# One more product of the last stage split into seven smaller products, and one more slice in seven of its weight sums added by transfers

## The chip, the cores and the metric

The kernel runs on one core of a Trainium2 chip. The metric is the device time of one execution in microseconds (us). TensorE (PE in the profile) multiplies, VectorE (DVE) adds and subtracts tensors, ScalarE (ACT) copies and applies functions, GpSimd (POOL) and SyncE (SP) here only issue transfers (DMAs).

## What is computed

The reference is a gated mix of two branches over a 2048 x 1024 input. Branch a is the real part of a two-dimensional Fourier transform, written as matrix products. Branch b is a token-mixing MLP: LayerNorm, a product with w1 (2048 x 3584), GELU, a product with w2 (3584 x 2048), with biases. A sigmoid gate of each row mixes them.

```python
g = sigmoid((x * gate_w).sum(-1, keepdims=True))
a = real(dft_seq @ (x @ dft_hid.T))
h = layernorm(x)
u = gelu(einsum("bsd,sf->bdf", h, w1) + b1)
b = transpose(einsum("bdf,fs->bds", u, w2) + b2)
return g * a + (1 - g) * b
```

The change touches the product with w2 alone, the last stage.

## The kernel before, in words

The kernel runs four stages one after the other: two for the Fourier branch (`FastSeq`, `FastHid`), then `Up` (the product with w1 and the GELU) and `Down` (the product with w2, line 1384). It keeps float32 accuracy by splitting each operand into a high part `hi` and a rest `lo`, both of the format fp32r, and by multiplying three times: hi by hi, hi by lo and lo by hi. ACT makes `hi` (line 666), DVE makes `lo` as the difference (line 673, or line 671 where the sign of the operand is turned at the same time). A plain matmul is 128 x 128 weights by 512 columns (lines 1069 to 1071).

`Up` and `Down` are of the class `Bilinear` (line 740). The matrices are cut in blocks: in `Down` the weights w2 (called W) are 4 x 4 blocks of 896 x 512, the stored result u of `Up` (called R) is 4 x 2 blocks of 896 x 512, and the output is 4 x 2 blocks. A fixed table, `SCHEME`, computes the 32 block products as 26 products of signed sums of blocks. `O_ORDER` (line 244) gives the order of the 26 products; product j here is the j-th in that order. `plan` chooses by which additions the sums are made and which sums stay in SBUF for the next products (`O_KEEP`) or go to a buffer in HBM.

One product has seven slices k of 128 rows (`nk` = 7), four groups m of 128 output rows (`nm` = 4) and 512 columns: 7 x 4 x 3 = 84 matmuls. Its result stands in four PSUM banks, which DVE or ACT then read into accumulators (`read`; lines 1114 and 1122). A product can be chained to the one before, and then goes on in the same banks.

Two tuples and a method steer what the change is about:

- `O_NEST` (line 282) lists the products that are made in the nested way (`nested`, line 921): the first six of the seven slices form a 2 x 2 scheme of quarters, which takes seven smaller products in place of eight. Each of the seven has three slices, two groups of output rows, 256 columns and three passes: 18 matmuls of 256 columns. ACT first writes zeros into the halves of the banks that begin an accumulation (`zero`, line 967), copies two halves (line 987), and DVE adds shared halves in PSUM (line 992). The operands of the seven are quarters or sums of quarters: four sums of three quarter-slices for R (names `_s`) and four for W (names `_t`), and each operand is split into hi and lo. The seventh slice is done in the plain way. Before the change, products 3, 15 and 22 are nested.
- `by_dma` (line 1393) says which block sums are made by a transfer that adds, in place of an addition on DVE. It holds for products j above 1 in the slices k with (k + j) mod 7 in `O_DMA` (line 278), and for all slices of the products in `O_MADE` (line 279). `operand` (line 845) uses it where one of the two terms is still in HBM, the other may be overwritten, and the signs agree: the other term stays where it lies, and `add_onto` (line 641) issues on POOL a DMA that adds the first one onto it. Otherwise both terms are loaded by SP (line 639) and DVE adds or subtracts (lines 631 and 634).

The order of all instructions is not written by hand. `Graph.schedule` places each task on its engine by its own cost figures, by due times that it takes from the order of TensorE's work, and by free slots: `SLOTS` gives 39 buffers of 4 KB per partition ("f"), 24 of 2 KB ("h") and 8 PSUM banks. The order found when the kernel is built is fixed; each engine then runs its list in that order and waits on semaphores. So each engine can be ahead of TensorE as far as buffers, loads and its own speed allow.

Of the kernel before, what the change touches and what calls it, by code (L numbers as in the profile page):

```python
# [274 lines left out]


O_KEEP, O_AHEAD = 2, 7
O_DMA = (1, 4, 6)
O_MADE = (3, 6, 9, 21, 22, 23)
U_MADE = (0, 1)  # L280
O_GAP = 99
O_NEST = (3, 15, 22)
O_CLOSE = ((0, 6), (0, 7), (0, 9), (1, 7), (1, 10), (1, 12), (1, 13), (1, 20), (1, 22), (2, 2), (2, 5), (2, 12), (2, 13), (2, 14), (2, 18), (2, 21), (2, 23), (3, 1), (3, 2), (3, 3), (3, 4), (3, 8), (3, 9), (3, 13), (3, 15), (3, 19), (3, 20), (4, 1), (4, 4), (4, 18), (4, 19), (4, 20), (5, 0), (5, 7), (5, 10), (5, 15), (5, 17), (5, 20), (5, 22), (6, 1), (6, 4), (6, 7), (6, 9), (6, 11), (6, 13), (6, 15), (6, 18), (6, 19))
Y_NEST = ()
O_PERM = ((0, 1, 2, 3), (0, 1, 2, 3), (0, 1))
# [277 lines left out]
def arm(  # L563
# [176 lines left out]
    class Bilinear:  # L740
# [90 lines left out]
        def by_dma(self, x, j, k, o):  # L831
            return False
# [551 lines left out]
    class Down(Bilinear):  # L1384
        pairs = True
        nest, close = O_NEST, O_CLOSE
        gap = O_GAP
# [5 lines left out]
        def by_dma(self, x_, j, k, o):  # L1393
            return j > 1 and (k + j) % 7 in O_DMA or j in O_MADE

# [1057 lines left out]
```

## Time and profile before

| what | value |
|---|---|
| time, median of 3 runs | 1230.14 us (1228.32 to 1230.95) |
| the profiled execution's own time | 1229.13 us |
| span in its profile | 1227.3 us (1.8 us lie around it) |
| granted TensorE clock | 0.999 |
| TensorE busy | 1212.1 us, 99% of the span |
| DVE busy | 1150.9 us, 94% |
| ACT busy | 703.7 us, 57% |
| POOL busy | 210.4 us, 17% |
| first and last matmul of `Down` | 725.6 us and about 1219 us |

A row of the profile's groups names the line, the engine, the operation, what is written and read (buffer numbers left out), the shape and the count, then busy time and mean duration. In the timeline a row is a start and a duration in us; in square brackets stands how long the engine was idle before it and what released it. Rows in the timeline that follow each other on one engine can overlap: the spacing of their starts says how fast the engine takes such instructions. Names that begin with `o_` or `ps_o` belong to `Down`, with `u_` or `ps_u` to `Up`.

### The profile page before, as it was taken

The page shows a single profiled execution, that of the slowest core. Times are in us where ns is not written, and L with a number is a line of the kernel's source. Part 1 is how long each engine was busy: PE and PEld are TensorE (multiplying, and loading weights), DVE is VectorE, ACT ScalarE, POOL GpSimd, SP SyncE. Part 2 cuts the span into 40 slices and gives each one's busy share as a digit, 9 for nine tenths or more (in the row PEclk, how much of TensorE's full clock was granted, in tenths as well). Part 3 has the DMA queues.
Part 4 walks back from the last instruction along what each step waited for, and adds up shares of the span by engine and source line. Part 5 has one row for each costly group of instructions (what it writes and reads, how often), then busy time and mean ns, then how long its engine had stood idle before and what let it go on. Part 6 is the DMA issues. An engine that isn't in the chain of part 4 may idle for free.

```text
span 1227.3 us, 17616 instructions
## 1 busy us (share of the span) xinstructions
PE 1212.1 (99%) x5640; PEld 979.4 (80%) x5647; DVE 1150.9 (94%) x1989; ACT 703.7 (57%) x1262; POOL 210.4 (17%) x325
## 2 busy tenths in 40 slices
PE   9999999999999999999999999999999999999997
PEld 6578756778888888888887878988888889888986
DVE  8999979999998899979999899899999889999995
ACT  8852699565843434645656556655535546765632
POOL 0000010312130221312312132102110112231302
PEclk9999999999999999999999999999999999999999
DMA  9999882989587799999998999778984678899655
GB/s 374 403 335 408 289 254 92 292 295 380 200 285 267 261 355 394 367 408 409 415 379 312 396 398 275 216 235 223 258 269 143 169 186 230 232 260 282 134 133 106
DMA packets 142281, 347.35 MB, mean 283 GB/s; under 512 B 17377, under 2 KB 20321, under 8 KB 142178
## 3 DMA queue, kind: packets, MB, share of 16 engines
q1 hardware_dynamic: 109762, 256.39, 58.0%
q0 software_dynamic: 32272, 89.67, 26.6%
q8 instruction: 46, 0.75, 0.3%
q14 instruction: 57, 0.47, 0.1%
q10 hardware_dynamic: 144, 0.07, 0.0%
HBM read 264.40 MB, written 81.66 MB: 282 GB/s over the span
## 4 chain that ended last, share of the span: by engine, by line


## 5 line engine op out<-in xcount | busy, mean ns | idle before, releaser
L1071 PE MATMUL ps_u_p<-u_p_r_hi,u_p_w_lo 128*128 128x512 f32 x728 | 283.5, 389 | 1.8 <-DVE u_p_w_lo L671 1.8
L1070 PE MATMUL ps_u_p<-u_p_r_lo,u_p_w_hi 128*128 128x512 f32 x728 | 283.3, 389 | 1.2 <-DVE u_p_r_lo L673 1.2
L1069 PE MATMUL ps_u_p<-u_p_r_hi,u_p_w_hi 128*128 128x512 f32 x728 | 283.7, 390 | 0.3 <-DVE u_c L1122 0.2
L1069 PE MATMUL ps_o_p<-o_p_r,o_p_w 128*128 128x512 f32 x654 | 255.0, 390 | 0.6 <-DVE u_c L1122 0.6
L1070 PE MATMUL ps_o_p<-o_p_r,o_p_w 128*128 128x512 f32 x654 | 254.5, 389 | 0.0
L1071 PE MATMUL ps_o_p<-o_p_r,o_p_w 128*128 128x512 f32 x654 | 254.4, 389 | 0.0
L1071 PEld LDWEIGHTS ps_u_p<-u_p_r_hi,u_p_w_lo 128*128 128x128 f32 x728 | 136.7, 188 | 31.1 <-DVE u_p_w_lo L671 2.7
L1070 PEld LDWEIGHTS ps_u_p<-u_p_r_lo,u_p_w_hi 128*128 128x128 f32 x728 | 136.7, 188 | 29.6 <-DVE u_p_r_lo L673 1.6
L1069 PEld LDWEIGHTS ps_u_p<-u_p_r_hi,u_p_w_hi 128*128 128x128 f32 x728 | 136.7, 188 | 29.4 <-DVE u_c L1122 1.1
L666 ACT ACTIVATE u_p_w_hi<-u_W_p 128x896 fp32r<-128x896 f32 x104 | 97.9, 950 | 105.9 <-DVE u_W_p L631 33.3
L1069 PEld LDWEIGHTS ps_o_p<-o_p_r,o_p_w 128*128 128x128 f32 x654 | 122.8, 188 | 28.2 <-DVE u_c L1122 1.9
L666 ACT ACTIVATE o_p_r<-o_R_p 128x512 fp32r<-128x512 f32 x157 | 96.5, 626 | 84.8 <-DVE o_R_p L634 39.8
L1071 PEld LDWEIGHTS ps_o_p<-o_p_r,o_p_w 128*128 128x128 f32 x654 | 122.8, 188 | 25.4
L1070 PEld LDWEIGHTS ps_o_p<-o_p_r,o_p_w 128*128 128x128 f32 x654 | 122.8, 188 | 25.1
L666 ACT ACTIVATE o_p_w<-o_W_p 128x512 fp32r<-128x512 f32 x164 | 100.6, 625 | 61.1 <-DVE o_W_p L634 28.3
L673 DVE TENSOR_TENSOR o_p_r<-o_R_p,o_p_r 128x512 fp32r<-128x512 f32 x157 | 106.4, 683 | 2.2 <-ACT o_p_r L666 2.2
L1122 DVE SCALAR_TENSOR_TENSOR u_c<-ps_u_p,u_c 128x512 f32<-128x512 f32 x161 | 104.7, 683 | 1.1 <-PE ps_u_p L1071 0.7
L649 POOL DMA_DIRECT2D u<-u_c x126 | 68.7, 545 | 198.7 <-DVE u_c L1122 111.1
L1623 PE MATMUL ps_fq<-fc,fx_f 128*128 128x256 f32 (+1 forms) x368 | 100.3, 417 | 2.2 <-DVE fx_f L631 2.1
L644 POOL DMA_DIRECT2D o_W_p<-in_w_dram x50 | 45.3, 930 | 266.1 <-DVE o_p_w L671 68.0
L1623 PEld LDWEIGHTS ps_fq<-fc,fx_f 128*128 128x128 f32 x368 | 69.4, 190 | 26.4 <-issue 12.4
L631 DVE TENSOR_TENSOR u_W_p<-u_W_p,u_W_p 128x896 f32<-128x896 f32 x72 | 76.7, 1085 | 10.9 <-DMA u_W_p<-in_w_dram 10.8
(291 smaller groups left out, 1982.8 us busy)
## 6 DMA issues: line engine op xcount, KB each, us to landing
u_W_p<-in_w_dram SPq DMA_DIRECT2D x124, 448.0 KB, 7.9
o_W_p<-in_w_dram SPq DMA_DIRECT2D x160, 256.0 KB, 5.8
o_R_p<-u SPq DMA_DIRECT2D x140, 256.0 KB, 5.7
fc<-in_ct_dram SPq DMA_DIRECT2D x64, 512.0 KB, 9.2
u<-u_c POOLq DMA_DIRECT2D x126, 256.0 KB, 6.4
u_c<-u SPq DMA_DIRECT2D x70, 256.0 KB, 8.5
o_W_p<-in_w_dram POOLq DMA_DIRECT2D x50, 256.0 KB, 6.9
out_dram<-o_c POOLq DMA_DIRECT2D x44, 256.0 KB, 7.9
```

The costliest lines, as they stand in the source:

```text
L631: g.add({"DVE": dve(o.n)}, key, lambda e: nc.vector.tensor_add(o.ap, a.ap, b.ap), r=(a.reg, b.reg), w=(o.reg,))
L644: g.add({"POOL": 0.9}, key, lambda e: nc.gpsimd.dma_start(dst(), src, accum_op=ALU.add), r=(v.reg, *r), w=(v.reg,), nbytes=2.2 * P * v.n * 4)
L649: g.add({queue: 0.6 if queue == "POOL" else 0.06}, key, lambda e: q.dma_start(dst, v.ap), r=(v.reg,), w=(reg,) if reg else (), nbytes=P * ...
L666: g.add({"ACT": act(v.n)}, key, lambda e: nc.scalar.activation(hi.ap, v.ap, AF.Copy, scale=-1.0 if negate else 1.0), r=(v.reg,), w=(hi.reg,))
L673: nc.vector.tensor_sub(lo.ap, v.ap, hi.ap.bitcast(F32))
L1069: nc.tensor.matmul(bank.ap, wh.ap[:, c], rh.ap[:, e], start=a, stop=False, skip_group_check=True)
L1070: nc.tensor.matmul(bank.ap, wh.ap[:, c], rl.ap[:, e], start=False, stop=False, skip_group_check=True)
L1071: nc.tensor.matmul(bank.ap, wl.ap[:, c], rh.ap[:, e], start=False, stop=b, skip_group_check=True)
L1122: lambda e: nc.vector.scalar_tensor_tensor(o.ap, ps.ap, scale, o.ap, op0=ALU.mult, op1=ALU.add),
L1623: nc.tensor.matmul(b.ap[:, c0:c0 + r.shape[-1]] if r.shape[-1] < H else b.ap, w, r, start=begin, stop=end, skip_group_check=True)
```

## The change

```diff
-O_DMA = (1, 4, 6)
+O_DMA = (1, 3, 4, 6)
...
-O_NEST = (3, 15, 22)
+O_NEST = (0, 3, 15, 22)
```

Product 0, the first one of `Down`, becomes nested like products 3, 15 and 22. Its operands are single blocks: W block 9 and R block 2, with no block sums. And in the products that `by_dma` covers by slice, four slices of seven are asked to be made by adding transfers, where it was three. No other line differs; the order of all engines' work is found anew from the same rules.

## The prediction

> **What bounds the kernel now.** I read the page first: the span and the busy time of the engines.
>
> ```profile
> span 1227.3 us, 17616 instructions
> ...
> PE 1212.1 (99%) x5640; PEld 979.4 (80%) x5647; DVE 1150.9 (94%) x1989; ACT 703.7 (57%) x1262; POOL 210.4 (17%) x325
> ```
>
> TensorE is busy nearly always, DVE almost as long. The page's chain that ended last is empty here, so I go by stretches of the last stage: the 22.6 us before its first matmul, products 0 to 2, product 3 up to 960 us, then the rest. The columns are the length, then busy time and instructions of PE, weight loads, DVE, ACT and POOL, the clock, the share of the DMA engines and GB/s.
>
> ```profile
> 703.00:725.60 22.60, 22.60 (x102) 18.64 (x101) 20.74 (x35) 7.37 (x13) 4.88 (x10) 1.00 1.04 391
> 725.60:784.40 58.80, 58.17 (x253) 46.98 (x253) 54.95 (x106) 39.58 (x78) 14.30 (x21) 1.00 0.89 277
> 784.40:960.00 175.60, 175.60 (x834) 147.68 (x834) 174.26 (x290) 96.17 (x170) 22.20 (x28) 1.00 0.75 220
> 960.00:1012.00 52.00, 52.00 (x231) 43.05 (x230) 43.79 (x82) 22.26 (x41) 7.79 (x9) 1.00 0.75 193
> 1012.00:1219.00 207.00, 206.98 (x1034) 176.48 (x1033) 197.66 (x348) 120.94 (x220) 48.45 (x55) 1.00 0.79 201
> ```
>
> PE never waits in the last stage except at its start (58.17 of 58.80), so PE's own work sets the end. But DVE has 1.3 us of idle time in the 175.6 us from 784.4 on, and 8.2 us in the 52 us after that. It is a second bound just behind the first. ACT has room everywhere; the DMA engines are full (1.04) until PE begins the stage.
>
> How far DVE is ahead of PE decides what more DVE work costs. Product 3 is nested and its operands have names of their own (`_s`, `_t`, `_hi`, `_lo`), so its rows can be told apart. First the timeline of PE: the first matmul of the stage and the thirteenth, the first of product 3 and the first one behind its nested part, and two matmuls 33 apart in plain products.
>
> ```profile
> 725.59 0.39 PE L1069 MATMUL ps_o_p<-o_p_r,o_p_w 128*128 128x512 f32 x1
> ...
> 729.80 0.39 PE L1069 MATMUL ps_o_p<-o_p_r,o_p_w 128*128 128x512 f32 x1
> ...
> 784.44 0.28 PE L980 MATMUL ps_o_p<-o_p_r_hi,o_p_w_hi 128*128 128x256 f32 x1
> ...
> 799.55 0.40 PE L1069 MATMUL ps_o_p<-o_p_r,o_p_w 128*128 128x512 f32 x1
> ...
> 1187.57 0.39 PE L1069 MATMUL ps_o_p<-o_p_r,o_p_w 128*128 128x512 f32 x1
> ...
> 1195.05 0.39 PE L1069 MATMUL ps_o_p<-o_p_r,o_p_w 128*128 128x512 f32 x1
> ```
>
> Then DVE's timeline: its first work for the stage, its waits, and how fast it takes instructions.
>
> ```profile
> 703.00 2.50 DVE L673 TENSOR_TENSOR o_p_w<-o_W_p,o_p_w 128x512 fp32r<-128x512 f32 x4
> ...
> 712.10 0.69 DVE L631 TENSOR_TENSOR o_W_p<-o_W_p,o_W_p 128x512 f32<-128x512 f32 x1 [0.82 <-DMA o_W_p<-in_w_dram]
> ...
> 719.24 0.69 DVE L634 TENSOR_TENSOR o_R_p<-o_R_p,o_R_p 128x512 f32<-128x512 f32 x1 [0.88 <-DMA o_R_p<-u]
> ...
> 730.06 0.68 DVE L671 SCALAR_TENSOR_TENSOR o_p_w<-o_W_p,o_p_w 128x512 fp32r<-128x512 f32 x1
> ...
> 742.70 0.68 DVE L671 SCALAR_TENSOR_TENSOR o_p_w<-o_W_p,o_p_w 128x512 fp32r<-128x512 f32 x1
> ...
> 753.53 0.68 DVE L673 TENSOR_TENSOR o_p_r<-o_R_p,o_p_r 128x512 fp32r<-128x512 f32 x1
> 754.13 0.68 DVE L673 TENSOR_TENSOR o_p_w<-o_W_p,o_p_w 128x512 fp32r<-128x512 f32 x1
> ...
> 757.75 1.08 DVE L631 TENSOR_TENSOR o_p_r_s<-o_R_p,o_R_p 128x256 f32<-128x256 f32 x3
> 758.75 1.09 DVE L634 TENSOR_TENSOR o_p_w_t<-o_W_p 128x256 f32<-128x256 f32 x3
> ...
> 763.79 0.94 DVE L673 TENSOR_TENSOR o_p_r_lo<-o_p_r_s,o_p_r_hi 128x768 fp32r<-128x768 f32 x1
> 764.66 0.94 DVE L673 TENSOR_TENSOR o_p_w_lo<-o_p_w_t,o_p_w_hi 128x768 fp32r<-128x768 f32 x1
> ...
> 773.95 0.69 DVE L631 TENSOR_TENSOR o_W_p<-o_W_p,o_W_p 128x512 f32<-128x512 f32 x1 [0.78 <-DMA o_W_p<-in_w_dram]
> 775.21 0.69 DVE L631 TENSOR_TENSOR o_W_p<-o_W_p,o_W_p 128x512 f32<-128x512 f32 x1 [0.56 <-DMA o_W_p<-in_w_dram]
> ...
> 784.03 0.96 DVE L673 TENSOR_TENSOR o_p_w_lo<-o_p_w_t,o_p_w_hi 128x768 fp32r<-128x768 f32 x1 [2.50 <-PE ps_o_p L1071]
> 784.90 1.09 DVE L673 TENSOR_TENSOR o_p_r_lo<-o_R_p,o_p_r_hi 128x256 fp32r<-128x256 f32 x3
> ```
>
> DVE begins product 3's operands at 757.75, 26.7 us before PE begins the product. The last one, the quarter for the last of the seven smaller products, is ready at 784.90 + 1.09 = 786.0. PE wants it six smaller products after 784.44: the nested part takes 799.55 - 784.44 = 15.11 us, a seventh is 2.16, so at 784.44 + 12.95 = 797.4. DVE is 11.4 us ahead there. Product 1 turns the sign of its W operands: its seven W splits are the seven L671 rows from 730.06 to 742.70, so its last one is ready at 743.4. PE wants it with the sixth slice of product 1. Product 0 ends at 729.80 + 72 x 0.2267 = 746.1 (the pace is worked out below), five slices of 2.72 go before, so at 759.7: DVE is 16.3 us ahead.
>
> **PE's part.** A plain matmul of 512 columns is taken every (1195.05 - 1187.57) / 33 = 0.2267 us. Six plain slices are 72 matmuls, 16.32 us. Nested they are 7 x 18 = 126 matmuls of 256 columns in 15.11 us, 0.120 each. So product 0's matmuls get shorter by 1.2 us and no more: an eighth of the multiplying is saved, but half the columns cost 53% of the time. The Trainium skill, "TensorE: Matmul & The Clock Gate", section "Back-to-back issue gap", gives an isolated gap of columns / 2.4 + 2.5 ns, so an estimate of 215.8 and 109.2 ns: by it the nested form would save 15.54 - 13.76 = 1.8 us. The trace disagrees on the small matmul (120 ns), and the sum goes by the trace.
>
> At the start of the stage there is a second gain. From 725.59 to 729.80 stand 12 matmuls, which need 2.72 us and took 4.21: 1.5 us are lost while DVE reads the banks of the last product of `Up`. A plain product wants its four banks 0.68 us apart; the nested one works 18 matmuls (2.16 us) on two banks before it needs the third. Against that, ACT must write zeros into each bank once DVE has read it:
>
> ```profile
> L967 ACT ACTIVATE ps_o_p<-const-bfloat16-1.0 x12: 359/372/382, 729.6 to 1070.9; 128x256 f32<-128x256 bf16 x12
> ```
>
> That is 0.37 us and a hand-over more per bank. The three late banks were there 1.0, 2.2 and 3.4 us after the start; with 0.5 us more each they come at 1.5, 2.7 and 3.9, and are wanted at 1.1, 2.2 and 3.2. About 0.7 of the 1.5 us stays. Gain 0.8, bounds 0 and 1.5. PE's own part is -1.2 - 0.8 = -2.0 us.
>
> **DVE's part.** The counts behind the nested operands, over three nested products:
>
> ```profile
> L673 DVE TENSOR_TENSOR o_p_w_lo<-o_p_w_t,o_p_w_hi 128x768 fp32r<-128x768 f32 x12 | 11.4, 946 | 2.5 <-PE ps_o_p L1071 2.5
> ...
> L673 DVE TENSOR_TENSOR o_p_w_lo<-o_W_p,o_p_w_hi 128x256 fp32r<-128x256 f32 x27 | 10.1, 412 | 0.0
> ```
>
> So one nested product has 4 wide and 9 quarter splits for W and as many for R, and by the code 4 x 3 sums for each, and 4 additions in PSUM. By the spacing of starts three 256-wide instructions take 1.00 us (757.75 to 758.75) and a 768-wide one 0.87 (763.79 to 764.66). Sums 24 x 0.335 = 8.0, quarter splits 18 x 0.335 = 6.0, wide splits 8 x 0.87 = 7.0, in PSUM 4 x 0.335 = 1.3: 22.4 us. It takes the place of 12 plain splits at 0.60 (753.53 to 754.13), 7.2 us. DVE gets 15.2 us more, all before or within the first product. ACT gets 18 quarter and 8 wide `hi` splits in place of 12 plain ones:
>
> ```profile
> L666 ACT ACTIVATE o_p_w_hi<-o_p_w_t 128x768 fp32r<-128x768 f32 x12 | 10.1, 840 | 3.3 <-DVE o_R_p L634 2.3 <-DVE o_p_w_t L634 0.5 <-DVE o_p_r_lo L673 0.5
> ...
> L666 ACT ACTIVATE o_p_w_hi<-o_W_p 128x256 fp32r<-128x256 f32 x27 | 9.4, 405 | 0.3 <-PE ps_o_p L1071 0.3
> ```
>
> 18 x 0.405 + 8 x 0.84 = 14.0 us gross, and ACT is idle for 15.2 of the 22.6 us before the stage: no cost, unless ACT's work comes later than that.
>
> **The adding transfers.** I counted by the rule in `operand`, product by product; the same count for the kernel before gives 160 W loads and 50 adding W transfers, as the rows below have them. After, there are 12 more adding transfers (61 for W, one for R), 12 fewer sums on DVE, 11 fewer W loads and one reload less. DVE saves 12 x 0.60 = 7.2 us, spread thin: products 2 and 4 lose one sum each, product 5 two, products 8 and 10 one each, the other six lie from product 15 on.
>
> ```profile
> o_W_p<-in_w_dram SPq DMA_DIRECT2D x160, 256.0 KB, 5.8
> ...
> o_W_p<-in_w_dram POOLq DMA_DIRECT2D x50, 256.0 KB, 6.9
> ```
>
> An adding transfer must follow the load of the other term, so such a sum takes 5.8 + 6.9 us from the first issue, where two loads side by side and an addition took some 7. SP issues less and POOL 12 more; POOL is 17% busy. From product 2 on the DMA share is 0.75 to 0.89. I take no cost, and bound it by one late landing of 6.9 us less the lead of DVE, so again by DVE's lead.
>
> **What the lead pays.** For product 3's last operand: ready at 786.0 + 15.2 - 0.6 (product 2's sum) = 800.6, if DVE waits as before. PE wants it at 797.4 - 2.0 = 795.4. DVE's five waits on the way are 0.82 + 0.88 + 0.78 + 0.56 + 2.50 = 5.5 us. If a later DVE finds all of these loads landed and buffers free, it is ready at 795.1, in time by 0.3; if it keeps all five, PE waits 5.2. The three waits from 773 on I count as gone (DVE comes 10 us later to them), of the two before 720 half: 4.7 us filled, 0.5 us of PE wait. Product 1 is nearer to safe: 16.3 - 15.2 - 2.0 plus the 1.7 us leaves 0.8. After product 3 DVE is nearly level with PE, and a hand-over that the lead used to hide is then seen. The nearest row is nested product 22, where PE lost time in the middle:
>
> ```profile
> 1150.48 0.28 PE L980 MATMUL ps_o_p<-o_p_r_hi,o_p_w_lo 128*128 128x256 f32 x1
> 1150.77 0.39 PE L980 MATMUL ps_o_p<-o_p_r_hi,o_p_w_hi 128*128 128x256 f32 x1
> 1150.99 0.28 PE L980 MATMUL ps_o_p<-o_p_r_lo,o_p_w_hi 128*128 128x256 f32 x1
> ```
>
> 0.29 and 0.22 in place of 0.12 twice, 0.27 us; for two such places, products 0 and 3, I take 0.5. Bounds: 0, and the 5.2 above. From there on six sums fewer and the 8.2 us idle after 960 give DVE its lead back, so nothing is added later.
>
> Sum: -2.0 + 0.5 + 0.5 = -1.0 us. On the profiled execution that is 1229.13 - 1.0 = 1228.1. That execution stands 1.0 below the median of the runs shown, 1230.14, so the forecast for the median is 1229.1. The measurement can tell about 0.2%, 2.5 us, from no change.
>
> **Rivals.** *DVE becomes the bound at the front of the stage.* For it: 15.2 us more work against 11.4 us of lead, and only 1.3 us of slack in the next 175. Against it: the waits that a later DVE can fill. It decides once more than 0.3 us of the five waits stay; with all five, -2.0 + 5.2 = +3.2, 1233.3. Slower. Chance 0.22, of which two thirds beyond 0.2%.
>
> *Buffers run out at the change of stages.* The nested product needs 28 full-size split buffers over its life in place of 12 for six plain slices, while `Up` still holds its own. The 28 loads of product 1 then come later: the DMA share is 1.04 there at 391 GB/s, so 0.67 us per 256 KB load, and 14 loads held back are 9.4 us. Of product 1's remaining 0.8 us nothing stays: +8.6 - 2.0 = +6.6, 1236.7. The trace shows no buffer wait of DVE before 784.03, which speaks against so much. Chance 0.06. The Trainium skill, "Perfetto Trace Analysis", section "Optimization Strategy", says that gaps which repeat on the engine that should be full can mean too little SBUF; no run here shows it yet.
>
> *All of the cover holds.* The 1.5 us at the banks vanish, no new wait comes, and the sums saved late take away the 0.27 us in product 22: -1.2 - 1.5 - 0.3 = -3.0, 1227.1. Chance 0.12, nearly all of it beyond 0.2%.
>
> The forecast case, -2.0 to +2.0, has 0.60. The change does what it says by the count above; I give nothing to the opposite.
>
> **The numbers.** Faster by over 0.2%: 0.10, from the third rival. Slower: two thirds of 0.22 and most of 0.06, some of the forecast's upper edge, 0.24. Within: 0.66. The range reaches from the third rival, 1227.1 less a little for the spread of the runs, 1226.8, to the first rival's 1233.3 and a little more, 1234.5; the second is left out.
>
> **What would show it.** In the changed profile there should be 504 matmuls of 256 columns at line 980, the first of them at the start of the stage, and 15.1 us until line 1069 follows; 61 adding W transfers; 12 fewer DVE sums at lines 631 and 634; a gap at the first banks of 0.7 us. PE's waits between 745 and 800 should be about 1 us in sum. If they are 4 us or more with DVE named, the first rival is right; if DVE itself waits there for loads or for PE, the second. DVE should be idle for less than 3 us in the 52 us before product 15. The forecast is wrong if the stage starts later than 725.6: then `Up` was disturbed, which no term here holds.

## The result, and the profile after

| what | before | after |
|---|---|---|
| time, median | 1229.80 us (4 runs, 1228.32 to 1230.95) | 1241.84 us (4 runs, 1237.77 to 1242.40) |
| ratio | | 1.0094 [1.0074, 1.0115] |
| profiled execution, span | 1229.13, 1227.3 us | 1242.40, 1240.5 us |

The change makes the kernel slower by 0.94%. The forecast was a gain of 1.0 us, 1229.1, with a range from 1226.8 to 1234.5; the sign was wrong, and the time lies above the range. Here is the page of the kernel after, span and engines:

```profile
span 1240.5 us, 17800 instructions
...
PE 1215.7 (98%) x5701; PEld 984.7 (79%) x5701; DVE 1159.1 (93%) x2019; ACT 712.0 (57%) x1284; POOL 220.2 (18%) x337
```

TensorE's busy time grows by 3.6 us and the span by 13.2, so most of the loss is waiting, which the shares of the page do not show. DVE has 8.2 us more work, close to the 15.2 - 7.2 = 8.0 of the prediction, and 30 instructions more: nested operands bring 24 + 18 + 8 + 4 = 54 in place of 12, and 12 sums go. The DMA issues of the same page answer to the two rows of the prediction:

```profile
o_W_p<-in_w_dram SPq DMA_DIRECT2D x149, 256.0 KB, 6.0
...
o_W_p<-in_w_dram POOLq DMA_DIRECT2D x61, 256.0 KB, 7.4
```

The counts are those forecast, 11 loads fewer and 11 adding transfers more, and each lands a little later (6.0 and 7.4 us in place of 5.8 and 6.9).

Next the windows of the kernel after: the 24.9 us ahead of the stage, then nested product 0, the plain ones after it, nested product 3, plain ones, nested 15, and the rest. The columns are as in the prediction.

```profile
703.00:727.90 24.90, 24.90 (x111) 20.62 (x110) 18.67 (x40) 7.98 (x17) 3.24 (x6) 1.00 0.88 328
727.90:749.06 21.16, 17.18 (x128) 16.67 (x126) 19.92 (x40) 15.80 (x34) 4.83 (x9) 0.92 0.81 281
749.06:790.07 41.01, 41.01 (x183) 33.72 (x181) 40.69 (x78) 27.90 (x54) 12.07 (x16) 1.00 0.93 250
790.07:806.37 16.30, 15.37 (x128) 15.17 (x127) 14.31 (x32) 12.48 (x27) 1.73 (x2) 1.00 0.80 224
806.37:1018.59 212.22, 212.22 (x939) 175.63 (x937) 204.01 (x345) 107.29 (x190) 34.30 (x42) 1.00 0.78 220
1018.59:1038.92 20.33, 17.01 (x127) 16.70 (x126) 19.05 (x41) 15.14 (x32) 1.73 (x2) 0.92 0.49 162
1038.92:1231.23 192.31, 192.31 (x914) 161.74 (x912) 181.63 (x316) 107.80 (x193) 49.66 (x57) 1.00 0.82 199
```

All that TensorE loses in the stage lies in three nested products. Product 0 takes 21.16 us, product 3 takes 16.30 and product 15 takes 20.33, where a nested part took 15.11 before. The plain products between them have no wait at all. And in two rows the granted clock is 0.92. TensorE's timeline in the kernel after shows where:

```profile
727.90 0.28 PE L980 MATMUL ps_o_p<-o_p_r_hi,o_p_w_hi 128*128 128x256 f32 x1
...
732.09 0.28 PE L980 MATMUL ps_o_p<-o_p_r_hi,o_p_w_lo 128*128 128x256 f32 x1
733.75 0.39 PE L980 MATMUL ps_o_p<-o_p_r_hi,o_p_w_hi 128*128 128x256 f32 x1 [1.38 <-ACT ps_o_p L987]
...
736.05 0.28 PE L980 MATMUL ps_o_p<-o_p_r_hi,o_p_w_lo 128*128 128x256 f32 x1
738.93 0.58 PE L980 MATMUL ps_o_p<-o_p_r_hi,o_p_w_hi 128*128 128x256 f32 x1 [2.60 <-DVE ps_o_p L992]
739.31 0.41 PE L980 MATMUL ps_o_p<-o_p_r_lo,o_p_w_hi 128*128 128x256 f32 x1
739.52 0.41 PE L980 MATMUL ps_o_p<-o_p_r_hi,o_p_w_lo 128*128 128x256 f32 x1
...
742.22 0.28 PE L980 MATMUL ps_o_p<-o_p_r_hi,o_p_w_hi 128*128 128x256 f32 x1
...
797.50 0.28 PE L980 MATMUL ps_o_p<-o_p_r_hi,o_p_w_lo 128*128 128x256 f32 x1
798.71 0.39 PE L980 MATMUL ps_o_p<-o_p_r_hi,o_p_w_hi 128*128 128x256 f32 x1 [0.93 <-DVE ps_o_p L992]
...
1024.94 0.28 PE L980 MATMUL ps_o_p<-o_p_r_hi,o_p_w_lo 128*128 128x256 f32 x1
1028.54 0.38 PE L980 MATMUL ps_o_p<-o_p_r_hi,o_p_w_hi 128*128 128x256 f32 x1 [3.32 <-DVE ps_o_p L992]
```

Matmuls start 0.12 us apart, and what the distance has beyond that is lost. At 732.09 it is 1.54 us, at 736.05 it is 2.76, at 797.50 it is 1.09, at 1024.94 it is 3.48. The releaser in the brackets is no operand: it is ACT's copy from one half bank to the other (line 987) or DVE's sum in PSUM (line 992). Behind 738.93 the matmuls start 0.21 us apart, until 742.22. The windows of the wait and of this stretch say why (the clock is the column before the last two):

```profile
736.20:738.90 2.70, 0.13 (x2) 0.00 (x0) 2.70 (x7) 2.70 (x9) 0.30 (x1) 0.96 1.01 368
738.90:742.20 3.30, 3.27 (x15) 3.27 (x16) 3.30 (x9) 2.14 (x5) 0.00 (x0) 0.51 1.04 411
```

After the wait TensorE is granted half its clock (0.51) for 3.3 us. Thirteen matmuls there take 0.094 us too long each, 1.2 us. The same happens to 15 matmuls after 1028.54, 1.4 us.

The sum of the stage: product 0 is 21.16 - 15.11 = 6.05 us too long, product 3 is 1.19, product 15 is 5.2 (20.33 - 15.13). Against that stand the 1.5 us at the first banks, which are gone (the matmuls from 727.90 on follow each other), 1.2 for the smaller matmuls of product 0, and 0.4 in product 22. That makes +9.3; the stage from its first matmul to the end of its last is 503.33 us in place of 494.17, +9.2. Then 2.3 us are lost ahead of the stage (727.90 in place of 725.59), and 1.7 behind the last matmul (9.3 to the end of the span in place of 7.6).

Last, DVE's timeline in the kernel after, waits ahead of the stage and the rows that TensorE's waits named:

```profile
705.71 0.69 DVE L634 TENSOR_TENSOR o_R_p<-o_R_p,o_R_p 128x512 f32<-128x512 f32 x1 [0.93 <-DMA o_R_p<-u]
707.05 0.69 DVE L631 TENSOR_TENSOR o_W_p<-o_W_p,o_W_p 128x512 f32<-128x512 f32 x1 [0.65 <-DMA o_W_p<-in_w_dram]
...
712.72 0.42 DVE L673 TENSOR_TENSOR o_p_r_lo<-o_R_p,o_p_r_hi 128x256 fp32r<-128x256 f32 x1 [1.49 <-ACT o_p_r_hi L666]
...
714.86 0.93 DVE L631 TENSOR_TENSOR o_p_r_s<-o_R_p,o_R_p 128x256 f32<-128x256 f32 x2 [0.84 <-DMA o_R_p<-u]
...
738.44 0.43 DVE L992 TENSOR_TENSOR ps_o_p<-ps_o_p,o_p_shared 128x256 f32<-128x256 f32 x1
...
797.89 0.77 DVE L992 TENSOR_TENSOR ps_o_p<-ps_o_p,o_p_shared 128x256 f32<-128x256 f32 x2 [1.99 <-PE ps_o_p L980]
...
1010.79 0.69 DVE L631 TENSOR_TENSOR o_W_p<-o_W_p,o_W_p 128x512 f32<-128x512 f32 x1 [5.79 <-DMA o_W_p<-in_w_dram]
```

Between 702 and 720 DVE's waits add up to 6.3 us, where in the kernel before they were 0.82 + 0.88 = 1.7. But the kernel before has one more just ahead, which the kernel after has not:

```profile
700.79 1.09 DVE L673 TENSOR_TENSOR u_p_w_lo<-u_W_p,u_p_w_hi 128x896 fp32r<-128x896 f32 x1 [3.81 <-ACT u_p_w_hi L666]
```

With it the waits from 660 to 720 us are 5.5 us before and 6.3 after: they moved and hardly grew. From 718 to 743 DVE has none, and does the sum that TensorE waits for only at 738.44, with other work queued right ahead of it. At product 3 it is the other way round. DVE stood idle for 1.99 us, waiting for TensorE, and then did its two sums in one go (x2), after the whole of the third smaller product. In the kernel before, other work stood between the two sums, and the first began at 790.03, 1.1 us before the second. So the 1.09 us there are the hand-over itself and no late DVE; behind such a pair TensorE has the same idle time, 0.93 us, in e1, e2, e5 and e6. That the pairing makes it was not tested.

### The profile page after: what moved, and what is told of

Same layout as the page of the kernel before. It is cut to its first block, busy times and chain, and to the rows that moved or that the text cites. A ratio compares the mean times of both kernels' runs of the same rounds, so it can differ in the third digit from the quotient of the medians.

```text
span 1240.5 us, 17800 instructions
## 1 busy us (share of the span) xinstructions
PE 1215.7 (98%) x5701; PEld 984.7 (79%) x5701; DVE 1159.1 (93%) x2019; ACT 712.0 (57%) x1284; POOL 220.2 (18%) x337
## 4 chain that ended last, share of the span: by engine, by line
## 5 line engine op out<-in xcount | busy, mean ns | idle before, releaser
L1069 PE MATMUL ps_o_p<-o_p_r,o_p_w 128*128 128x512 f32 x630 | 245.3, 389 | 0.0
L1070 PE MATMUL ps_o_p<-o_p_r,o_p_w 128*128 128x512 f32 x630 | 245.1, 389 | 0.0
L1071 PE MATMUL ps_o_p<-o_p_r,o_p_w 128*128 128x512 f32 x630 | 245.1, 389 | 0.0
L1069 PEld LDWEIGHTS ps_o_p<-o_p_r,o_p_w 128*128 128x128 f32 x630 | 118.3, 188 | 25.2 <-ACT o_c L1114 0.3
L1071 PEld LDWEIGHTS ps_o_p<-o_p_r,o_p_w 128*128 128x128 f32 x630 | 118.3, 188 | 24.7
L1070 PEld LDWEIGHTS ps_o_p<-o_p_r,o_p_w 128*128 128x128 f32 x630 | 118.3, 188 | 24.0
L666 ACT ACTIVATE o_p_w<-o_W_p 128x512 fp32r<-128x512 f32 x158 | 96.1, 625 | 69.7 <-DVE o_W_p L634 22.9
L666 ACT ACTIVATE o_p_r<-o_R_p 128x512 fp32r<-128x512 f32 x151 | 91.5, 626 | 64.3 <-DVE o_R_p L634 44.7
L644 POOL DMA_DIRECT2D o_W_p<-in_w_dram x61 | 56.1, 976 | 275.2 <-DVE o_p_w L671 81.4
L673 DVE TENSOR_TENSOR o_p_r<-o_R_p,o_p_r 128x512 fp32r<-128x512 f32 x151 | 102.9, 686 | 0.6 <-ACT o_p_r L666 0.6
L631 DVE TENSOR_TENSOR u_W_p<-u_W_p,u_W_p 128x896 f32<-128x896 f32 x72 | 76.8, 1088 | 10.1 <-DMA u_W_p<-in_w_dram 10.1
```

Source lines behind the costliest of these rows:

```text
L631: g.add({"DVE": dve(o.n)}, key, lambda e: nc.vector.tensor_add(o.ap, a.ap, b.ap), r=(a.reg, b.reg), w=(o.reg,))
L644: g.add({"POOL": 0.9}, key, lambda e: nc.gpsimd.dma_start(dst(), src, accum_op=ALU.add), r=(v.reg, *r), w=(v.reg,), nbytes=2.2 * P * v.n * 4)
L666: g.add({"ACT": act(v.n)}, key, lambda e: nc.scalar.activation(hi.ap, v.ap, AF.Copy, scale=-1.0 if negate else 1.0), r=(v.reg,), w=(hi.reg,))
L673: nc.vector.tensor_sub(lo.ap, v.ap, hi.ap.bitcast(F32))
L1069: nc.tensor.matmul(bank.ap, wh.ap[:, c], rh.ap[:, e], start=a, stop=False, skip_group_check=True)
L1070: nc.tensor.matmul(bank.ap, wh.ap[:, c], rl.ap[:, e], start=False, stop=False, skip_group_check=True)
```

## The experiments

The kernel before was timed beside each: 1228.75 us beside e1 to e4, 1229.94 beside e5 to e8, 1229.62 beside e9 to e12, 1229.77 beside e13 to e15. The ratios go by these.

### The two halves of the change: e1 and e2

e1 takes the nested product alone, e2 the transfers alone.

```diff
 e1:  O_NEST = (0, 3, 15, 22)   O_DMA = (1, 4, 6)
 e2:  O_NEST = (3, 15, 22)      O_DMA = (1, 3, 4, 6)
```

> Product 0 nested, the adding transfers as before. Theory A (lag at the front): the nested product needs its R slices early, DVE waits some 6 us for them before the stage, and the additions in PSUM come late, so TensorE waits about 5 us in products 0 and 3 and its clock drops after the longest wait; product 15 goes without a wait of its own, since its 3.5 us came from a DVE wait of 5.8 us for a load of product 16 that stood among more adding transfers. 1235 to 1238 us. Theory B (transfers): the adding transfers crowd the DMA engines and make all loads late, the nested product alone is harmless: at most 1230 us.

> Four slices of seven by adding transfers, product 0 plain. Theory A: DVE is 15 us ahead of TensorE, so later loads are covered and 12 fewer sums change nothing: 1228.5 to 1231 us, no TensorE wait over 0.5 us in the last stage. Theory B: loads come late everywhere, TensorE waits as in the changed kernel: 1236 us or more.

e1: 1239.48 us, ratio 1.0083 [1.0066, 1.0100]. e2: 1231.00, ratio 1.0015 [1.0004, 1.0025]. The nested product is nearly all of it. In e1 TensorE waits in the same places: 1.32 us for ACT's copy, 2.76 for DVE's sum, and 2.89 in product 15, the last two followed by 13 and 16 matmuls at half clock. So the wait in product 15 does not need the added transfers, as I had thought when I saw DVE's 5.79 us at 1010.79, and e1 came out above the 1238 that I had expected without it. What e2 adds, 1.8 us by the ratio, is less than the 0.2% that I can tell from nothing. Its profile has one wait of TensorE above 0.5 us, which I had excluded: 0.93 us at 1151.90, in product 22, for a pair of DVE's sums. One part may be at the end: in the six kernels with the four slices (after, e2, e3, e5, e6, e9) the span goes on for 8.0 to 9.5 us behind the last matmul, in all others for 7.1 to 7.6, though the last store of the output lands 3.0 to 3.1 us behind it both before and after. What fills the rest was not sought.

### The wait that the plan does not know: e3 and e8

The fourth of the seven smaller products writes the left halves of two banks. DVE's sum at line 992, which it waits for, reads the right halves of the same banks. Its own operands were ready at 728.5, ten microseconds before it began. The planner tracks halves, so it sees no such wait and can put the sum behind other work. e3 (after) and e8 (before) tell it that such a product takes the whole bank:

```diff
-  g.add({"PE": 0.36 * kk}, key, go, r=(rh.buf, rl.buf, wh.buf, wl.buf), w=(ps.reg,))
+  g.add({"PE": 0.36 * kk}, key, go, r=(rh.buf, rl.buf, wh.buf, wl.buf), w=(ps.buf,))
```

> The changed kernel, with the planner told that a smaller product waits for the whole PSUM bank and not for its half alone; what is computed is the same. Theory C: all four long waits of TensorE stand at the fourth smaller product, whose own operands were ready, and end with the addition in PSUM of the other half of the same bank, which DVE's list holds back since the planner does not know of the wait. Told so, it puts the additions earlier: the waits there fall from 8.9 us to under 3 us and the time to 1231 to 1236 us. Rival D: DVE is simply behind, so the order in its list moves the wait to other operands: 1240 us or more.

> The kernel before, where the planner is told that a smaller product of a nested one occupies the whole bank (in the kernel after this gave a ratio of 1.005 in place of 1.0094). If the declaration mends a wait that only the change brought out, it does nothing here: within 1.5 us of before. If it is a gain by itself, the time is 1 to 3 us below before, and what the change costs is then larger by as much.

e3: 1234.38 us, ratio 1.0050 [1.0034, 1.0067], 7.5 less than after. The wait in product 15 is gone, the one at 797 is 0.61; in product 0 stay 0.96, 0.59 and 1.97 us. e8: 1229.10, ratio 0.9988 [0.9978, 0.9997]: no more than 0.12% for the kernel before, where DVE was far enough ahead. So, taken alone, the hidden wait costs the kernel after 7.5 us, and the kernel before next to nothing: the change took the lead that covered it. Of the versions that compute everything, e8 is the only one below the kernel before, by less than the 0.2% that I can tell from nothing.

The Trainium skill, "PSUM — Partial Sum Buffer", section "PSUM bank collisions raise a hardware error", says to guard PSUM by bank and not by address, since two engines must not touch one bank together even at different columns. The trace agrees in so far as TensorE stood for 2.60 us with its operands ready until DVE had left the other half of the bank.

### What a wait costs beyond itself: e4 and e7

The kernel before, with the first sum in PSUM of product 15 repeated, 11 times (e4) or 5 times (e7):

```diff
-  lambda e, v=v, x=x, y=y: nc.vector.tensor_add(v.ap, x.ap, y.ap)
+  lambda e, v=v, x=x, y=y, k=11 if (j, v) == (15, banks["V"][0]) else 1: [
+      nc.vector.tensor_add(v.ap, x.ap, y.ap) for _ in range(k)]
```

> The kernel before, with the first addition in PSUM for product 15 made eleven times over (the same sum each time), some 3.4 us more on DVE just where TensorE waits for it. If a wait of TensorE over 2.7 us is followed by a stretch at half clock, as after the two longest waits of the changed kernel, TensorE takes 256-column matmuls every 0.21 us in place of 0.12 for some 3.5 us and the time is 3.4 + 1.6 = 5 us above that of the kernel before; if the slow stretch there had another cause, 3.4 us or less.

> The kernel before, with the first of the sums in PSUM of product 15 done five times, so that PE waits once for about 1.7 us more (the same thing eleven times gave a wait of 4.43 us and behind it 23 matmuls at 0.213 in place of 0.120 us). If a half-clock stretch follows every wait, the time is 1.7 + about 1.4 above before: +3.1 us. If it needs a wait of more than 2 us, there is no matmul at 0.213 behind it and the time is +1.7 us.

TensorE in e4, then its windows, then TensorE in e7:

```profile
1017.89 0.28 PE L980 MATMUL ps_o_p<-o_p_r_hi,o_p_w_lo 128*128 128x256 f32 x1
1022.44 0.58 PE L980 MATMUL ps_o_p<-o_p_r_hi,o_p_w_hi 128*128 128x256 f32 x1 [4.27 <-DVE ps_o_p L993]
1022.82 0.41 PE L980 MATMUL ps_o_p<-o_p_r_lo,o_p_w_hi 128*128 128x256 f32 x1
1023.03 0.41 PE L980 MATMUL ps_o_p<-o_p_r_hi,o_p_w_lo 128*128 128x256 f32 x1
```

```profile
1017.90:1022.40 4.50, 0.27 (x3) 0.06 (x1) 4.19 (x11) 2.78 (x6) 0.00 (x0) 0.84 0.36 117
1022.40:1027.70 5.30, 5.26 (x24) 5.26 (x25) 4.05 (x9) 1.65 (x3) 0.00 (x0) 0.50 0.65 201
```

```profile
1020.21 0.28 PE L980 MATMUL ps_o_p<-o_p_r_hi,o_p_w_lo 128*128 128x256 f32 x1
1021.97 0.39 PE L980 MATMUL ps_o_p<-o_p_r_hi,o_p_w_hi 128*128 128x256 f32 x1 [1.48 <-DVE ps_o_p L993]
1022.19 0.28 PE L980 MATMUL ps_o_p<-o_p_r_lo,o_p_w_hi 128*128 128x256 f32 x1
1022.31 0.28 PE L980 MATMUL ps_o_p<-o_p_r_hi,o_p_w_lo 128*128 128x256 f32 x1
```

e4: 1235.48 us, 6.7 above before. A wait of 4.43 us and 23 matmuls at 0.213 us (2.2 us lost) make 6.6. e7: 1231.86, 1.9 above. A wait of 1.64 us, and from the second matmul on 0.12 us again. So here the short wait cost itself, and the long one half as much again. What decides between the two is in the last section.

### Is DVE late, or has it too much to do? e5 and e6

e5 takes product 0's R slices from the other half of the same rows, stored about 90 us earlier; e6 leaves out the 28 block sums of product 1.

```diff
 e5:
-  src, r = self.source(x, b, k)
+  src, r = self.source(x, b + (self.name + x == "oR" and j == 0), k)
 e6:
+  if (self.name, j) != ("o", 1):
       (add if ca * sa == cb * sb else sub)(key, v, va, vb)
```

> The kernel after, but product 0 takes its R slices from block 3 (the other half of the same rows), which was stored about 90 us earlier, in place of block 2, the result of the last-but-one product of Up. The output is not the reference's; the work is the same. Theory L (late slices): in the kernel after DVE stands idle for 6.3 us between 702 and 718 us, mostly because product 0's R slices are written to HBM just before they are wanted, and that is the room which I had counted as filled. Then DVE's idle time there falls below 2.5 us, the waits of product 0 (1.5 and 2.75 us, and the half-clock stretch behind the second) fall below 1 us in sum, and the time is 1234 to 1238. Theory B (plain backlog: 15 us more DVE work is more than any lead there was): product 0's waits get shorter by under 1 us and the time stays at 1240 to 1243.

> The kernel after without the 28 block sums of product 1 on DVE (the loads stay, the first term is used in place of the sum, so the output is not the reference's): 28 x 0.6 = 17 us less DVE work, part of it queued ahead of product 0's last operands and of its sums in PSUM. Theory B: DVE's amount of work is what is wrong: all of product 0's waits and the 1.1 us at 797 go, 1233 to 1236. Theory L: product 0's first operands are still late because the R slices are, and the wait for ACT's copy at 732 (1.5 us) stays, while the wait for the sum in PSUM (2.75) and the one at 797 go: 1235 to 1239, with the DVE idle time before 718 unchanged at 5 us or more.

e5: 1234.44 us, ratio 1.0035 [1.0024, 1.0047]. In DVE's timeline there is one wait between 700 and 720, at the beginning, which the kernel before has too (3.81 us at 700.79); in TensorE's the two waits of product 0 are there still, but shorter:

```profile
700.09 1.09 DVE L673 TENSOR_TENSOR u_p_w_lo<-u_W_p,u_p_w_hi 128x896 fp32r<-128x896 f32 x1 [4.08 <-ACT u_p_w_hi L666]
```

```profile
730.37 0.38 PE L980 MATMUL ps_o_p<-o_p_r_hi,o_p_w_hi 128*128 128x256 f32 x1 [1.02 <-ACT ps_o_p L987]
...
734.49 0.39 PE L980 MATMUL ps_o_p<-o_p_r_hi,o_p_w_hi 128*128 128x256 f32 x1 [1.71 <-DVE ps_o_p L992]
```

The last split of product 1 is ready at 755.4, 8 us sooner than in the kernel after (763.4), and product 15 waits for nothing. So without the late slices 7.4 of the 12 us go, and the time is the one that theory L gave. It does not follow that the slices alone are worth so much: e3 gained as much with DVE's waits as they were (6.2 us between 702 and 718 in its trace). And the waits in product 0, which it put below 1 us in sum, are 1.18 + 1.87 us: something else is late there too.

e6: 1231.70, ratio 1.0015 [1.0005, 1.0024]. ACT's copy is in time, DVE's sum is late by 1.27 us. TensorE in e6:

```profile
725.10 0.28 PE L981 MATMUL ps_o_p<-o_p_r_hi,o_p_w_hi 128*128 128x256 f32 x1
...
731.45 0.28 PE L981 MATMUL ps_o_p<-o_p_r_hi,o_p_w_lo 128*128 128x256 f32 x1
732.84 0.39 PE L981 MATMUL ps_o_p<-o_p_r_hi,o_p_w_hi 128*128 128x256 f32 x1 [1.12 <-DVE ps_o_p L993]
...
741.58 0.40 PE L1070 MATMUL ps_o_p<-o_p_r,o_p_w 128*128 128x512 f32 x1
```

Its nested part takes 741.58 - 725.10 = 16.5 us, 15.2 without the wait. That is TensorE's part of the forecast, seen in the rows. DVE's idle time in front of the stage fell to 2.1 us here, which I had expected to stay at 5 or more: with the sums gone the loads come in another order too. The time lies below what either theory gave (1233 at the least): with 17 us less work for DVE 10.1 of the 12 us go, more than with either mend, so the amount of work seems to count at least as much as the late slices. But e6 does not tell lateness and amount apart as cleanly as it was meant to.

### Both mends together: e9 and e12

e9 is e3 and e5 in one; e12 is e3 with the old three slices.

```diff
 e9, e12:  w=(ps.reg,)  ->  w=(ps.buf,)
 e9:       self.source(x, b, k)  ->  self.source(x, b + (self.name + x == "oR" and j == 0), k)
 e12:      O_DMA = (1, 4, 6)
```

> The kernel after with two of the edits that each took off 7.4 us: the whole bank declared for a smaller product, and product 0's R slices taken from a block stored earlier (the output is not the reference's). Theory LC (late slices make DVE late, and a late DVE is felt through the sum in PSUM; two links of one chain): with both, the waits in product 0 fall from about 3 us with either to 1 us or less, and the time is 1229.5 to 1232. Theory B (either only shifts a backlog that has to be paid somewhere): the waits move behind product 0, to products 1 to 5 or 15, and the time stays at 1233.5 to 1235.5.

> Product 0 nested, the old three slices in seven, the whole bank declared; everything computed. It is the kernel after with that declaration (1234.4 us) less the adding transfers. If the transfers cost what they cost alone (0.15%, 1.8 us), it is 1232 to 1233. If they relieve DVE where its lead is used up, it is slower than 1234.4. Whether it is below the kernel before (1229.9) decides if nested product 0 can pay at all without other data: I expect not.

e9: 1234.04 us, ratio 1.0032 [1.0020, 1.0043]. The two mends do not add up: each alone gave 1234.4. My theory LC, by which product 0's waits would fall to 1 us, is wrong; they are 0.91 and 1.87 us, at the same two matmuls. The other one had the time right, but not the place: nothing moved to later products. What is left is in product 0 itself. DVE's rows there have no gap from 702 to 740: Up's last bank reads, each with a sum of product 1 between, then product 0's own late operands, and the sum in PSUM behind them at 735.18.

e12: 1234.45 us, ratio 1.0028 [1.0017, 1.0039]. That is 0.2% below e3's ratio (1.0050), as e2 has it from the other side, but the two intervals meet and the medians are equal, so it settles nothing about the transfers. It stays above the kernel before, as expected. TensorE's waits in product 0 are 1.33, 1.52 and 1.48 us there, with 22 matmuls at half clock.

### TensorE's part alone: e10, e11, e13, e14

e10 and e11 are the nested and the plain kernel with whole banks, three slices and without product 1's sums; e13 and e14 take the R slices of products 0 and 1 from the block stored earlier as well.

```diff
 all:       O_DMA = (1, 4, 6)   w=(ps.reg,)  ->  w=(ps.buf,)
            if (self.name, j) != ("o", 1):  (add if ...)(key, v, va, vb)
 e10, e13:  O_NEST = (0, 3, 15, 22)
 e11, e14:  O_NEST = (3, 15, 22)
 e13, e14:  self.source(x, b, k)  ->  self.source(x, 3 if self.name + x == "oR" and j < 2 else b, k)
```

> Product 0 nested, the old three slices in seven by adding transfers, the whole bank declared, and the 28 block sums of product 1 left out (the output is not the reference's): DVE has its lead back, so that PE's part of the change stands alone. If my PE part was right (-1.2 for the matmuls, -0.8 to -1.5 at the banks), this is 2.0 to 2.7 us below the next kernel, which has the same edits without the nesting. If something in the nested product itself costs PE time (zeros, copies, pace), the two are within 1 us.

> The control to the one before: the kernel before with the whole bank declared and the 28 block sums of product 1 left out (the output is not the reference's). PE did not wait for DVE in the kernel before, so 17 us less DVE work should bring nothing by itself: within 1 us of the 1229.1 that the same kernel gave with these sums.

> Product 0 nested, the old three slices in seven, the whole bank declared, the 28 block sums of product 1 left out, and the R slices of products 0 and 1 taken from a block stored earlier (the output is not the reference's). Neither a late slice nor a backlog on DVE is left at the start of the stage. If my PE part was right, product 0's nested part takes 15.1 to 15.6 us, there is no wait at the stage's first banks, and the time is 2.0 to 2.7 us below the next kernel. If the hand-overs from PE to ACT to DVE and back inside a nested product are too tight at the change of stages whatever DVE has to do, product 0 still takes 17 us or more and the two are within 1 us.

> The control to the one before: the same edits with product 0 plain (the output is not the reference's). PE had no DVE wait there to lose: within 1 us of 1229.2, what the same kernel gave with the R slices where they belong.

| kernel | time | ratio to before | wait in product 0 |
|---|---|---|---|
| e10, nested | 1233.27 us | 1.0020 [1.0010, 1.0031] | 3.07 us |
| e11, plain | 1229.22 us | 0.9993 [0.9982, 1.0004] | none |
| e13, nested | 1233.98 us | 1.0043 [1.0030, 1.0057] | 3.91 us, then 13 matmuls at half clock |
| e14, plain | 1231.32 us | 1.0010 [1.0001, 1.0018] | none |

The nested kernel is not 2.0 to 2.7 us faster but 0.3% slower, and each time with one long wait at the same matmul. Two things limit the comparison. In both plain kernels the loss at the first banks is gone too (12 matmuls in 2.72 us, from 725.21 in e11 and from 726.26 in e14), so there only the 1.2 us of the smaller matmuls could be gained. And e14 is 2.1 us above e11, where I had expected at most 1. The chain in e13, ACT, DVE and then TensorE:

```profile
733.11 0.63 ACT L666 ACTIVATE o_p_r<-o_R_p 128x512 fp32r<-128x512 f32 x1 [3.44 <-DMA u<-u_c]
734.51 0.38 ACT L988 ACTIVATE o_p_shared<-ps_o_p 128x256 f32<-128x256 f32 x1 [0.78 <-DMA o_W<-o_W_p]
```

```profile
736.05 0.42 DVE L993 TENSOR_TENSOR ps_o_p<-ps_o_p,o_p_shared 128x256 f32<-128x256 f32 x1
```

```profile
732.51 0.28 PE L981 MATMUL ps_o_p<-o_p_r_hi,o_p_w_lo 128*128 128x256 f32 x1
736.54 0.58 PE L981 MATMUL ps_o_p<-o_p_r_hi,o_p_w_hi 128*128 128x256 f32 x1 [3.75 <-DVE ps_o_p L993]
```

Now it is ACT that stands still, for 3.44 us, in front of a split of product 0's seventh slice. What it waits for is a store of Up's result. The split reads and writes nothing of Up, so what is left is a buffer that they share: the 4 KB it is to write would still hold that result. The profile leaves buffer numbers out, so this is found by elimination. ACT works its list in order, so the copy for DVE's sum stands behind, and then waits 0.78 us for a buffer of its own. (In e10 I had taken the same wait of ACT, 2.41 us, for a late slice; e13 has no late slices, and it is there.) With late slices, backlog and the bank out of the way, buffers seem to be the next to bind, as my second rival had it, though TensorE pays for it at DVE's sum.

### Another place: e15

The kernel before with whole banks and product 6 nested in place of product 0.

```diff
-O_NEST = (3, 15, 22)
+O_NEST = (3, 6, 15, 22)
```

> The kernel before with the whole bank declared and product 6 nested in place of product 0, everything computed. Its operands come from blocks that were stored long before, its banks from the stage's own products. If the change of stages is what makes product 0 dear, this is 1228 to 1231 (-1.2 for the matmuls, +0 to +2 of hand-overs). If DVE's 15 us more cannot be carried anywhere in the first 235 us of the stage, where DVE is idle for 1.3 us in 175, PE waits 4 us or more in products 6 to 10 and it is 1232 to 1237, no better than product 0's 1234.4.

```profile
842.78:858.84 16.06, 15.34 (x128) 15.16 (x126) 15.77 (x34) 9.79 (x21) 2.70 (x5) 1.00 1.03 270
```

1231.44 us, ratio 1.0012 [1.0002, 1.0022]. The nested part takes 16.06 us with one wait of 0.88. That is between the two expectations: dearer than e8 (0.9988) by 0.24%, where product 0 (e12, 1.0028) is by 0.40%. So product 0 looks dearer than product 6, as it would if the change of stages made it so, but the two intervals meet, and this is not shown. A further nested product does not pay at this other place either. Only this one was tried.

## Why the prediction was wrong

- **The counts** were right: the same instructions came and went, and DVE's busy time grew by 8.2 us, 8.0 by the sum.
- **TensorE's part, -2.0,** was right, and a little small. The pace stayed 0.120 us, and of the 1.5 us at the first banks nothing stayed where I left 0.7. In e6 the nested part without its wait takes 15.2 us, where the six plain slices of the kernel before took 16.3 + 1.5 = 17.8. But no kernel here shows it as a time, since none had a nested product 0 without a wait.
- **"What the lead pays" is the step that failed**, and in three ways. Its 0.5 us of TensorE waits were 8.9 us, and 2.6 us of half clock besides. First, it took 4.7 us of DVE's 5.5 us of waits as filled by a later DVE. The three from 773 on did go. Ahead of the stage nothing was filled: with the 3.81 us at 700.79, which the prediction did not count, the waits were 5.5 us and became 6.3. The nested operands need product 0's R slices earlier than the plain ones did, and those leave Up last. Product 1's last split came at 763.4 in place of 743.4; less the 2.3 us by which the stage began later that is 17.7 us, not 15.2 less 1.7. What of the 12 us is due to the late slices, to the amount of work and to the hidden wait can't be told apart: taking each away alone brings 7.4 (e5), 10.1 (e6) and 7.5 us (e3), which is twice the whole.
- Second, it compared leads only where an **operand** is wanted. The first waits are for the copy and the sum inside the nested product, which no operand shows. By the code TensorE comes back to the bank nine matmuls, 1.1 us, after it has left the half that DVE's sum reads. In product 0 the sum must fit in there while DVE still clears Up's banks and makes later operands, and what stands ahead of it in DVE's list is paid by TensorE. I had priced such hand-overs at 0.5 us for two products, from product 22. They cost 1.54 + 2.76 + 1.09 + 3.48 = 8.9 us.
- Third, it knew no price for a wait **beyond its length**: 1.2 + 1.4 us at half clock in the profiled execution.
- **"Nothing is added later" failed too.** At product 14's last split DVE was 12.3 us behind its former time (995.90 in place of 983.56) and TensorE, at product 15, only 6.6, so the lead had not come back; product 15's hidden wait, 5.2 us with its half clock, is nearly as large as what product 0 lost.
- **The transfers** were taken at no cost; e2 has 1.8 us, which is too little to be sure of.
- **The rivals.** The first named the right engine and the right side, at +3.2 with a chance of 0.22. It went by the same five waits and the same operands, so it was too small by the same errors. The second, buffers, is not seen to bind in the kernel after; in e13 it is what is left by elimination.
- **The start of the stage** came at 727.90, which the prediction named as a sign of an effect it did not hold. About 1.7 us of the 2.3 are there already at Up's first matmul (227.12 in place of 225.44), behind a stretch of half clock in the first stage (0.91 from 40 to 60 us). The profiles of e1, e4, e8 and e9 have it too, the others, the kernel before among them, don't, all with the same work in the same order there, so it is not the change. The other 0.6 are lost between 650 and 675 us, inside Up. Product 0 need not be nested for such a start: in e15, where it is plain, the stage starts at 727.64.

What stays open: how large the gain of a nested product 0 would be with all four shortages gone, whether the adding transfers lose anything, and why a pair of sums in a row on DVE waits for the whole smaller product.

## What to carry to other kernels

A lead is spent at the first hand-over, not at the last operand: list every wait between engines inside the new part, with what is queued ahead of it on each, before calling its work hidden. Idle time of the second-busiest engine counts as room only if what it waits for does not move with the change. When a mend brings half and a second mend brings the same half again, look for the next shortage at the same instruction; what each mend brings alone can't be added up.

## What the runs showed of the hardware

The half clock was not in any term. The granted clock in the traces shows how it comes. It changes only at borders that stand whole multiples of 3.413 us apart in one trace: in the kernel after it falls at 738.69 and again at 1028.83, 85 x 3.413 us later. A stretch at half clock is one such window long, or two. Here are the windows on both sides of a border, first in the kernel after, where the wait of 2.60 us lies in one window, then in e10, where a border (counted back from the clock's fall at 1224.90, behind the last matmul) cuts the wait of 2.91 us in two.

```profile
735.28:738.69 3.41, 1.05 (x9) 0.85 (x8) 3.41 (x7) 3.41 (x10) 1.22 (x3) 1.00 0.99 359
738.69:742.11 3.42, 3.18 (x15) 3.18 (x16) 3.42 (x10) 2.35 (x5) 0.00 (x0) 0.50 1.04 413
```

```profile
729.97:733.39 3.42, 1.89 (x16) 1.69 (x15) 0.83 (x2) 1.20 (x3) 1.07 (x2) 1.00 0.96 335
733.39:736.80 3.41, 2.02 (x17) 2.03 (x18) 3.27 (x8) 3.41 (x8) 0.00 (x0) 1.00 1.01 384
```

The table has TensorE's idle times, its busy time in the window just ahead of the half clock (where none followed, in the emptiest windows around the wait), and what followed.

| kernel, place | idle before | busy in a window of 3.41 us | matmuls at 0.213 us behind it |
|---|---|---|---|
| e7, product 15 | 1.48 us | 2.02 us | none |
| e5, product 0 | 1.02 and 1.71 us | 2.41 and 1.85 us | none |
| e9, product 0 | 0.76 and 1.71 us | 2.42 and 2.30 us | none |
| e10, product 0 | 2.91 us | 1.89 and 2.02 us | none |
| e12, product 0 | 1.18, 1.36 and 1.18 us | 1.76 us, then 2.23 at half clock | 22 |
| e3, product 0 | 1.81 us, after 0.80 and 0.43 in the 5 us before | 1.60 us | 15 |
| after and e1, product 0 | 2.60 us | 1.05 and 0.96 us | 13 |
| e1, product 15 | 2.73 us | 0.93 us | 16 |
| after, product 15 | 3.32 us | 0.29 us | 15 |
| e13, product 0 | 3.75 us | 0.00 us | 13 |
| e4, product 15 | 4.27 us | 0.58 us, then 1.97 at half clock | 23 |

So a wait's length does not decide alone: 2.60 us brought the half clock, and 2.91 did not. In these rows it is how much of one window TensorE works: at full clock 1.76 us or less was followed by a window at half clock, 1.85 us or more was not. The limit is not as sharp elsewhere. In the first stage 1.57 us was followed by half clock in the kernel after, while 1.56 us in e7 was not; nor was 1.66 us at the end of e14.

The borders lie at other times in each execution, so the price of the same wait changes. Of the four executions of the kernel after, three have a granted clock of 0.992 or 0.993 and took 1241.40 to 1242.40 us. The fourth has 0.997, which leaves room for one half-clock window at most besides those at its end, and took 1237.77. From these times I estimate that some 4 of the 12 us are half clock, the stretch in the first stage included.

The Trainium skill, "TensorE: Matmul & The Clock Gate", section "HAM oscillation — how this bites in real kernels", gives gaps above some 3.4 us as the danger. Here 2.60 us was enough. The Trainium skill, "TensorE: Matmul & The Clock Gate", section "What's actually happening", describes a window of 3413 ns that runs freely and does not start anew with the kernel. The traces agree: the borders are 3.413 us apart, and the wait of e10 escaped because a border cut it. No run moved one and the same wait against the borders on purpose.
